# Delta-rule attention with two rational/Mish networks: weight conversion by scaled words in PSUM, and the rest of a redesign around it

## The chip, the cores and the metric

The kernel runs on one core of a Trainium2 chip. A core has TensorE (PE; its weight loads are listed as PEld), VectorE (DVE), ScalarE (ACT), GpSimd (POOL) and SyncE (SP), which issues most of the transfers; each works through its own queue in order. The metric is the device time of one execution in microseconds (us), lower is better. The input arrays lie in DRAM, the weights as 64-bit floats.

## The reference, cut

```python
k_n = k / (norm(k) + 1e-6)                       # B=4, H=8, S=768, D=48
for t in range(S):
    y[t] = q[t] @ state                          # state: 48x48 for each b, h
    state += beta[t] * outer(k_n[t], v[t] - state.T @ k_n[t])
x = y as (3072 tokens, 384)
h = x @ w_in;  P = a0 + a1*h + a2*h^2 + a3*h^3   # w_in 384x2048
x = (P / (1 + |b0|*|h| + |b1|*h^2 + 1e-6)) @ w_out
h = x @ w_in2; out = (h * tanh(log(1 + exp(h)))) @ w_out2
```

## The kernel before, in words

The sequence is cut into 24 chunks `u` of C=32 steps; four chunks make a token group G (0 to 5) of 512 tokens. A chunk needs a prepare: the keys' norms (L259), transposes of k and q (L309, copied at L313), their products (L321) and two masked products on VectorE (L327). For each G one triangular inverse follows for all four chunks: a transpose of `lg` into `xs` (L357), 30 steps of a product and a sum (L366, L372), on VectorE for G=0 and on GpSimd for the others (`ONPOOL`), a transpose into `xt` (L376) and a scaling by beta on GpSimd (L379). Then each chunk has a step: `ks` (L421), `uu` with `xt` (L433), two state products `s_mm(c)` (L450) with a VectorE sum each (L458), `y_mm` (L469), and a product that turns y into the networks' input `x` (L481 to L485). The steps are a chain through the state.

The networks' unit is a slice of 128 of the 2048 hidden columns for 512 tokens: (m, G, f), m the network, f 0 to 15. Each has nine `up` matmuls (L641), elementwise work, and nine `down` (L647; L656 in the last set), 128x128x512 in fp32r with every operand split in a high and a low word, and three products of these. There are 192 units, in sets of 16. In the first network five VectorE operations (L679, L680, L683, L684, L685) and two or three of GpSimd (L674, L678, L687) stand between `up` and `down`; in the second two Mish on ScalarE (L689, L690) and one subtraction on VectorE (L691).

A weight piece is one of 64: two networks, 16 slices, two sides. [...] `st` is stored to a DRAM scratch `wd` (L592) and fetched from there by every unit that needs it (L634), two fetches of 0.393 MB a unit.

The order on every engine is not written by hand. `Plan` collects operations with an estimated duration, the buffers that they read and write, and for units a due time. `order()` works back from the due times to a latest start for each (`late`, less the operation's `early`), then runs a small simulation in which each free engine takes the ready operation with the earliest `late`:

```python
late[j] = min(late[j], late[i] - p[1] - p[4] - self.HOP)
...
pick = min((x for x in queue if x[0] <= t), key=lambda x: (late[x[1]], x[1]))
```

Operations without a due time behind them come in program order. The main function adds the head (group 0's attention, then all conversions) and then sets: first network on G=0; then for g = 0, 1, 2 the steps of g+1, second network on g, prepare of g+2 with its inverse, first network on g+1, norms of g+3; and so on to the second network on the last two groups. `HOST` stretches the due times of units that share the time with steps.

## Time and profile before

| | |
|---|---|
| three runs | 1339.13, 1348.69, 1351.46 us; median 1348.69 |
| profiled execution | time 1342.18 us, span 1340.5 us, mean granted TensorE clock 0.913 |
| busy in the span | PE 1098.8 us (82%), PEld 873.9, DVE 713.5 (53%), ACT 586.1 (44%), POOL 570.8 (43%) |
| moved by transfers | 224.79 MB, mean 168 GB/s |

The span runs from the first to the last instruction of the profiled execution. A row of a window gives the busy time of each engine in that stretch of the span; a row of a line gives the busy time of one line's operations, the mean duration of one, and the idle time of the engine ahead of them with what ended it. A timeline row shows in brackets how long the engine had waited and for whom. PE's busy time counts matmuls in flight, so it is near the span where matmuls follow each other closely.

### The profile page before, as it was taken

The page shows a single profiled execution, that of the slowest core. Times are in us where ns is not written, and L with a number is a line of the kernel's source. Part 1 is how long each engine was busy: PE and PEld are TensorE (multiplying, and loading weights), DVE is VectorE, ACT ScalarE, POOL GpSimd, SP SyncE. Part 2 cuts the span into 40 slices and gives each one's busy share as a digit, 9 for nine tenths or more (in the row PEclk, how much of TensorE's full clock was granted, in tenths as well). Part 3 has the DMA queues.
Part 4 walks back from the last instruction along what each step waited for, and adds up shares of the span by engine and source line. Part 5 has one row for each costly group of instructions (what it writes and reads, how often), then busy time and mean ns, then how long its engine had stood idle before and what let it go on. Part 6 is the DMA issues. An engine that isn't in the chain of part 4 may idle for free.

```text
span 1340.5 us, 32163 instructions
## 1 busy us (share of the span) xinstructions
PE 1098.8 (82%) x13168; PEld 873.9 (65%) x13168; DVE 713.5 (53%) x1172; ACT 586.1 (44%) x1022; POOL 570.8 (43%) x699
## 2 busy tenths in 40 slices
PE   5177558558878899998997998979993799999986
PEld 4175336346666778776776776767772678888775
DVE  3957799987565672227832247631244467841211
ACT  2035456532237572237741267631261457752211
POOL 4123456893115693005891027780037745720000
PEclk9578688869899899999998999899997899999998
DMA  5466777677895666554864554753453346776562
GB/s 100 116 164 175 240 255 244 205 237 222 263 284 165 174 188 163 136 144 105 243 171 108 141 142 115 231 165 97 126 127 104 80 125 166 195 194 191 151 194 64
DMA packets 209283, 224.79 MB, mean 168 GB/s; under 512 B 134864, under 2 KB 147664, under 8 KB 209136
## 3 DMA queue, kind: packets, MB, share of 16 engines
q1 hardware_dynamic: 205616, 222.04, 59.4%
q8 instruction: 104, 1.70, 0.5%
q10 hardware_dynamic: 3264, 0.59, 0.3%
q14 instruction: 43, 0.35, 0.1%
q0 software_dynamic: 256, 0.10, 0.0%
HBM read 190.42 MB, written 29.88 MB: 164 GB/s over the span
## 4 chain that ended last, share of the span: by engine, by line
PE 45%; POOL 10%; DVE 9%; DMA 6%; SPq 6%; ACT 5%; issue 3%; DVEq 0%; POOLq 0%; ACTq 0%
PE b_h L641 18%; PE b_o L647 17%; SPq L719 4%; POOL xs L372 4%; POOL tmp L366 3%; PE b_t L450 3%; PE b_t L469 2%; DMA wd<-st 2%; DMA win<-wd 2%; DMA raw<-in_moe_w_in_dram 1%; PE b_t L433 1%; PE b_o L656 1%; POOL gh L687 1%; DVE b_r L684 1%; DMA out_dram<-ev 1%
## 5 line engine op out<-in xcount | busy, mean ns | idle before, releaser
L641 PE MATMUL b_h<-x,win 128*128 128x512 f32 x1728 | 461.5, 415 | 79.2 <-DVE ms L680 42.6
L647 PE MATMUL b_o<-gh,wout 128*128 128x512 f32 x1584 | 417.8, 411 | 66.2 <-POOL gh L687 41.4
L641 PEld LDWEIGHTS b_h<-x,win 128*128 128x128 f32 x1728 | 334.6, 198 | 165.0 <-DVE ms L680 50.8
L647 PEld LDWEIGHTS b_o<-gh,wout 128*128 128x128 f32 x1584 | 302.7, 196 | 145.2 <-POOL gh L687 49.2
L689 ACT ACTIVATE gh<-b_h 128x512 fp32r<-128x512 f32 x96 | 57.4, 598 | 272.3 <-PE b_h L641 266.7
L691 DVE TENSOR_TENSOR gh<-mq,gh 128x512 fp32r<-128x512 f32 x96 | 69.5, 728 | 179.9 <-ACT mq L690 177.2
L678 POOL TENSOR_TENSOR mq<-mq,mr 128x512 f32<-128x512 f32 x96 | 125.6, 1308 | 87.6 <-ACT mr L676 80.0
L687 POOL TENSOR_TENSOR gh<-mq,gh 128x512 fp32r<-128x512 f32 x96 | 125.1, 1304 | 65.2 <-ACT gh L686 51.0
L579 POOL TENSOR_TENSOR st<-wm,st 128x384 fp32r<-128x384 f32 x64 | 68.5, 1077 | 119.6 <-ACT st L576 100.2
L337 POOL TENSOR_TENSOR mb<-beta_t,mask 128x256 f32<-128x256 f32 x24 | 16.6, 690 | 241.4 <-DVE lg L327 241.2
L683 DVE SCALAR_TENSOR_TENSOR mq<-mq,b_r 128x512 f32<-128x512 f32 x96 | 65.4, 682 | 59.6 <-ACT b_r L682 57.0
L672 ACT ACTIVATE mq<-b_h 128x512 f32<-128x512 f32 x96 | 57.0, 593 | 90.8 <-PE b_h L641 64.0
L679 DVE TENSOR_TENSOR ms<-ms,b_h 128x512 f32<-128x512 f32 x96 | 65.2, 679 | 47.4 <-ACT ms L677 46.8
L372 POOL TENSOR_TENSOR xs<-xs,tmp 128x30 f32<-128x30 f32 (+9 forms) x150 | 82.0, 547 | 11.8
L670 ACT ACTIVATE mr<-mq,cst 128x512 f32<-128x512 f32 x96 | 69.1, 721 | 29.1 <-POOL mq L678 28.8
L366 POOL TENSOR_TENSOR tmp<-xs 128x30 f32<-128x30 f32 (+9 forms) x150 | 77.6, 518 | 8.6
L677 ACT ACTIVATE ms<-b_h,ab 128x512 f32<-128x512 f32 x96 | 73.9, 770 | 0.6 <-PE b_h L641 0.6
L680 DVE SCALAR_TENSOR_TENSOR ms<-ms,ab,b_h 128x512 f32<-128x512 f32 x96 | 71.2, 742 | 1.7
L684 DVE SCALAR_TENSOR_TENSOR b_r<-ms,ab,b_r 128x512 f32<-128x512 f32 x96 | 71.8, 748 | 0.0
L682 ACT ACTIVATE b_r<-mr 128x512 f32<-128x512 f32 x96 | 57.5, 599 | 28.8 <-DVE mq L685 27.7
L576 ACT CAST st<-wm 128x384 fp32r<-128x384 f32 x64 | 32.3, 509 | 80.4 <-DVE wm L569 48.6
L686 ACT CAST gh<-mq 128x512 fp32r<-128x512 f32 x96 | 58.7, 612 | 19.3 <-DVE mq L685 19.0
(124 smaller groups left out, 1350.0 us busy)
## 6 DMA issues: line engine op xcount, KB each, us to landing
win<-wd SPq DMA_DIRECT2D x192, 384.0 KB
wout<-wd SPq DMA_DIRECT2D x192, 384.0 KB
wd<-st SPq DMA_DIRECT2D x64, 384.0 KB
raw<-in_moe_w_out_dram SPq DMA_DIRECT2D x32, 384.0 KB
raw<-in_moe_w_in_dram SPq DMA_DIRECT2D x16, 384.0 KB
v<-in_v_dram SPq DMA_DIRECT2D x192, 24.0 KB
qn<-in_q_dram SPq DMA_DIRECT2D x92, 48.0 KB
kn<-in_k_dram SPq DMA_DIRECT2D x88, 48.0 KB
```

What stands on the lines that cost most here:

```text
L366: eng.tensor_tensor(out=tv, in0=xs[:, j, j + 1:C].unsqueeze(1).to_broadcast([128, j, n]), in1=xs[:, 0:j, j:j + 1].to_broadcast([128, j, n] ...
L372: eng.tensor_tensor(out=xs[:, 0:j, j + 1:C], in0=xs[:, 0:j, j + 1:C], in1=tv, op=ALU.add)
L579: nc.gpsimd.tensor_tensor(out=st[:, 1], in0=mf, in1=st[:, 0].bitcast(F32), op=ALU.subtract)
L641: nc.tensor.matmul(out=h, lhsT=win[:, a, j], rhs=x[:, c, slab[j]], start=n == 0, stop=n == 8)
L647: nc.tensor.matmul(out=self.banks[f"o{d}"], lhsT=wout[:, a, d], rhs=gh[:, c], start=first and j == 0, stop=last and j == 2,)
L670: act(out=r, in_=q, func=ACTF.Ln, bias=k["c"])
L677: p.add("ACT", 775, lambda: act(out=s, in_=h, func=ACTF.Identity, scale=k["a3"], bias=k["a2"]), [hb], [sb])
L678: p.add("POOL", 1335, lambda: P.tensor_tensor(out=q, in0=q, in1=r, op=ALU.mult), [rb], [qb])
L680: p.add("DVE", 750, lambda: V.scalar_tensor_tensor(out=s, in0=s, scalar=k["a1"], in1=h, op0=ALU.add, op1=ALU.mult), [hb], [sb])
L684: p.add("DVE", 750, lambda: V.scalar_tensor_tensor(out=rp, in0=s, scalar=k["a0"], in1=rp, op0=ALU.add, op1=ALU.mult), [sb], ["r"])
L687: p.add("POOL", 1320, lambda: P.tensor_tensor(out=gh[:, 1], in0=q, in1=gh[:, 0].bitcast(F32), op=ALU.subtract), [qb], [ghb])
L691: p.add("DVE", 755, lambda: V.tensor_tensor(out=gh[:, 1], in0=q, in1=gh[:, 0].bitcast(F32), op=ALU.subtract), [qb], [ghb])
```

## The change

**Pieces.** A piece's sign is made without taking it off and putting it back: the high word, read as a 32-bit float, is clamped on both sides, scaled by 2^-112 on ScalarE, and VectorE takes the maximum of the clamped word times -2^-80 and the scaled one. For a positive word that is the scaled one, for a negative one a positive number whose exponent is 32 higher; a shift left by three then moves that bit to the sign's place (`sign`, `shift`), and `tail` brings the low word's top bits. ScalarE's absolute value, VectorE's mask and one two-tensor operation go, the scaled word lies in a PSUM bank. `kind` says which way a piece goes: pieces without "v" are clamped on GpSimd and get their low part from two TensorE matmuls with an identity and its negative (`lo_mm`) and a ScalarE copy; pieces with "v" are clamped on VectorE, into the bank, and get the low part on GpSimd. The `fold` branch of `plan` (ScalarE's parametric ReLU) is not taken: every `kind` has an "m".

**Where pieces stand.** Twelve slices (`HEAD`) of the first network are converted in the head in bank `r`, four more and four of the second network (`EARLY`) in bank `t1` beside the first set, the rest in bank `r` beside the second set. Units 0 to 7 of the first set and all of the second read the converted tiles where they are made; only units 8 to 11 (`FETCHED`) and all later groups fetch them. Fetches fall from 384 to 328.

**Attention.** For G=0 the k part of the prepares stands ahead of the q part, the inverse works in a pair of PSUM banks (`solved`), and the state accumulates in PSUM so that ScalarE copies replace VectorE sums. For all groups `s_mm` is one group of 64 matmuls over four tile positions. The scaling by beta is split in four, one for each chunk. For G of 1 or more the inverse is planned a stage ahead of `finish`, which transposes and scales.

**Planner.** `HOP` depends on the engine, a TensorE change from small to wide tiles costs 150 ns in the plan, the first set's pace is 6500 ns, and GpSimd's and the steps' `early` differ for groups 0 and 1.

In the diff, cut to its core, removed lines that the listing above shows are left out.

```diff
+HEAD = 12
+FETCHED = range(8, 12)
+EARLY = 4
...
-RAW = 3
+RAW = 5
...
-    HOP = 110
+    HOP = {"PE": 180}
...
+            if "k" in what:
+                self.inverse(p, G)
+            if what == "k":
+                self.finish(p, G)
+                p.add("DVE", 980, lambda: self.nc.vector.memset(self.pair, 0.0), (), ["o0", "o1"])
...
+    def solved(self, G):
+        return (self.xs, ["xs"]) if G else (self.pair.rearrange("p (a b) -> p a b", a=C), ["o0", "o1"])
...
+    def finish(self, p, G):
...
+        def scale(g):
+            part = xt[:, g * M:g * M + M]
+            beta = self.beta_t[:, GU * G + g].unsqueeze(2).to_broadcast([128, M, C])
+            return lambda: eng.tensor_tensor(out=part, in0=part, in1=beta, op=ALU.mult)
+        p.add("DVE", 2070, last, xb, [f"xt{g}" for g in range(GU)], early=lead(AHEADX, G))
+        for g in range(GU):
+            p.add(engine, 690 if engine == "POOL" else 350, scale(g), (), [f"xt{g}"], early=lead(AHEADX, G))
...
+        def s_mm():
+            for m in range(M):
+                a, n = divmod(m, 4)
+                for e in (0, 3, 1, 2):
+                    r = self.srow(e)
+                    rows = slice(32 * e, 32 * e + 32)
+                    nc.tensor.matmul(
+                        out=self.banks[bs[e % 2]][r:r + 64, m * D:(m + 1) * D],
+                        lhsT=kn[rows, 2 * n + r // 64, :] if a == e // 2 else kns[rows, n, :],
+                        rhs=U[rows, m, :], start=G > 0, stop=True, skip_group_check=G == 0,
+                    )
...
+            p.add("PE", 1000, s_mm, ["U", knb, knsb], bs, early=lead(AHEAD, G))
             for c in range(2):
...
+                if G:
+                    p.add("DVE", 560, s_out(c), [bs[c], f"{sb}{c}"], [f"{tb}{c}"], early=lead(AHEAD, G))
+                else:
+                    p.add("ACT", 490, s_copy(c), [bs[c]], [f"{tb}{c}"], early=lead(AHEAD, G))
...
+        def clamp():
+            (nc.vector if "v" in kind else nc.gpsimd).tensor_scalar(
+                out=at, in0=high.bitcast(F32), scalar1=self.MOST, scalar2=-self.MOST, op0=ALU.min, op1=ALU.max,
+            )
...
+        def scale():
+            nc.scalar.activation(out=to, in_=at, func=ACTF.Identity, scale=self.DOWN)
+        def sign():
+            nc.vector.scalar_tensor_tensor(out=pv, in0=at, scalar=self.SIGN * self.DOWN, in1=to, op0=ALU.mult, op1=ALU.max)
         def shift():
             nc.vector.tensor_scalar(
...
+                out=ps, in0=ps if kind else m, scalar1=3, scalar2=None, op0=ALU.logical_shift_left,
+            )
+        def tail():
             nc.vector.scalar_tensor_tensor(
...
+                out=m, in0=low, scalar=29, in1=ps, op0=ALU.logical_shift_right, op1=ALU.bitwise_or,
...
+        def lo_mm():
+            nc.tensor.matmul(out=rest, lhsT=self.ident, rhs=v, start=True, stop=False)
+            nc.tensor.matmul(out=rest, lhsT=self.minus, rhs=split[:, 0].rearrange("p k c -> p (k c)"), start=False, stop=True)
+        def lo_copy():
+            nc.scalar.copy(out=split[:, 1].rearrange("p k c -> p (k c)"), in_=rest)
         p.dma(380 if side or self.n else 2500, 384, get, (), [rawb])
+        here, there = (bank, mb) if "v" in kind else (mb, bank)
+        if "v" in kind:
+            p.add("DVE", 520, clamp, [rawb], [here])
+        else:
+            p.add("POOL", 1490, clamp, [rawb], [here])
         if late:
...
+            p.add("ACT", 550, scale, [here], [there])
+            p.add("DVE", 580, sign, [mb], [bank])
+            p.add("DVE", 470, shift, (), [bank])
         else:
...
+        p.add("DVE", 550, tail, [rawb, bank], [mb])
+        p.add("ACT", 510, hi, [mb], [buf])
+        if "v" not in kind:
+            p.add("PE", 1000, lo_mm, [mb, buf], ["h1"], early=3000)
+            p.add("ACT", 520, lo_copy, ["h1"], [buf])
+        else:
+            p.add("POOL", 1060, lo, [mb], [buf])
+        p.dma(380, 384, lambda: nc.sync.dma_start(out=self.scratch[f][:, side], in_=split.bitcast(F32)), [buf], [f"wd{self.n}_{f}_{side}"])
...
+        if G or i in FETCHED:
+            p.dma(330, 384, fetch(0, win), [f"wd{m - 1}_{f}_0"], [winb], early=6000)
+            p.dma(330, 384, fetch(1, wout), [f"wd{m - 1}_{f}_1"], [woutb], early=6000)
...
+    def units(m, g, host, convert=lambda f: None):
+        nonlocal due
         for f in range(NF):
...
+            convert(f)
+            ml.plan_unit(plan, m, g, NG, f, NF, due)
+            due += (PACE if due > START + NF * PACE1 - 1 else PACE1) + HOST * host
+    def first(f):
+        for n in range(HEAD if f == 0 else 0):
+            ml.convert(plan, 1, n, "r", NF, SIGNS)
+        if 0 <= f - 5 < NF - HEAD:
+            ml.convert(plan, 1, HEAD + f - 5, "t1", NF, SIGNS + "v")
+        if 0 <= f - 12 < EARLY:
+            ml.convert(plan, 2, f - 12, "t1", NF, SIGNS + "v")
+    def second(f):
+        for n in (range(EARLY, 6) if f == 0 else (f + 5,)):
+            if n < NF:
+                ml.convert(plan, 2, n, "r", NF, "mv")
+    def prepare(g):
+        at.norms(plan, g)
+        at.prepares(plan, g)
+    units(1, 0, 0, first)
+    at.prepares(plan, 1)
+    at.finish(plan, 1)
+    at.norms(plan, 2)
+    for g in range(NG - 2):
+        at.steps(plan, g + 1)
+        units(2, g, 1, second if g == 0 else lambda f: None)
+        if g == 0:
+            at.prepares(plan, 2)
+        at.finish(plan, g + 2)
+        if g + 3 < NG:
+            at.norms(plan, g + 3)
+            at.prepares(plan, g + 3)
         else:
...
+            at.steps(plan, g + 2)
+        units(1, g + 1, g + 2 == NG - 1)
+    units(1, NG - 1, 0)
+    units(2, NG - 2, 0)
+    units(2, NG - 1, 0)
```

**Three places in the order.** On TensorE where the first `up` stands (`u_151` and `u_168` are the attention's U, `b_h` the networks' banks, `win` the weight tile). Before:

```order
L450 MATMUL b_o_101<-u_151,kns_137 64x48
L450 MATMUL b_o_101<-u_151,kn_127 64x48
L641 MATMUL b_h_98<-x_173,win_176 128x512 x9
L309 MATMUL b_t_105<-ident_120,kn_129 128x2x64 x4
L641 MATMUL b_h_99<-x_173,win_177 128x512 x9
L421 MATMUL b_t_104<-su_149,kq_142 32x48 x32
```

In the changed kernel the end of the fourth step's product into `x` comes first, then (`arena` and `gh` hold a piece's word and its parts):

```order
L543 MATMUL b_t_103<-ident_143,y_176 128x2x64 x2
L547 MATMUL b_t_103<-ident_143,y_176 64x64 x4
L658 MATMUL b_h_99<-arena,ident_143 128x384
L659 MATMUL b_h_99<-gh_133,minus 128x384
L353 MATMUL b_t_102<-ident_143,kn_147 128x2x64 x4
L760 MATMUL b_h_98<-x_112,win_115 128x512 x9
L658 MATMUL b_h_99<-arena,ident_143 128x384
L659 MATMUL b_h_99<-gh_134,minus 128x384
L353 MATMUL b_t_102<-ident_143,qn_148 128x2x64 x4
L658 MATMUL b_h_99<-arena,ident_143 128x384
L659 MATMUL b_h_99<-gh_135,minus 128x384
L760 MATMUL b_h_99<-x_112,win_116 128x512 x9
```

The `up` at L760 now has 22 pairs of `lo_mm` (L658, L659) ahead of it and two more pairs between the first and the second `up`; before it followed the step directly, with the first transposes of the next group behind it.

On VectorE in the middle of the second network's first set (`wm` and `raw` are the piece's tiles, L691 is a unit's subtraction). Before:

```order
L549 TENSOR_SCALAR wm_113<-raw_110 128x384
L554 TENSOR_SCALAR wm_113<-wm_113 128x384
L559 TENSOR_SCALAR wm_113<-wm_113 128x384
L564 SCALAR_TENSOR_TENSOR wm_113<-raw_110,wm_113 128x384
L569 SCALAR_TENSOR_TENSOR wm_113<-raw_110,wm_113 128x384
L549 TENSOR_SCALAR wm_114<-raw_111 128x384
L554 TENSOR_SCALAR wm_114<-wm_114 128x384
L559 TENSOR_SCALAR wm_114<-wm_114 128x384
L564 SCALAR_TENSOR_TENSOR wm_114<-raw_111,wm_114 128x384
L569 SCALAR_TENSOR_TENSOR wm_114<-raw_111,wm_114 128x384
L691 TENSOR_TENSOR gh_195<-mq_185,gh_195 128x512
```

The changed kernel there (L624 clamp, L635 sign, L638 shift, L643 tail, L811 the unit's subtraction, L444 a transpose of the inverse):

```order
L624 TENSOR_SCALAR b_r<-arena 128x384
L444 STREAM_TRANSPOSE xt_173<-xs_172 128x32x32
L635 SCALAR_TENSOR_TENSOR b_r<-b_r,arena 128x384
L638 TENSOR_SCALAR b_r<-b_r 128x384
L643 SCALAR_TENSOR_TENSOR arena<-arena,b_r 128x384
L624 TENSOR_SCALAR b_r<-arena 128x384
L635 SCALAR_TENSOR_TENSOR b_r<-b_r,arena 128x384
L638 TENSOR_SCALAR b_r<-b_r 128x384
L643 SCALAR_TENSOR_TENSOR arena<-arena,b_r 128x384
L624 TENSOR_SCALAR b_r<-arena 128x384
L811 TENSOR_TENSOR gh_137<-mq_123,gh_137 128x512
L635 SCALAR_TENSOR_TENSOR b_r<-b_r,arena 128x384
```

A piece has four operations where it had five, all through one bank `b_r`, and a clamp often stands directly ahead of the sign of the same piece, with ScalarE's scaling between them.

On GpSimd around the inverse of group 5 (L366 and L372 its steps, L687 the low part `gh` that a `down` reads). Before, its end:

```order
L366 TENSOR_TENSOR tmp_157<-xs_155 128x58
L372 TENSOR_TENSOR xs_155<-xs_155,tmp_157 128x29x2
L366 TENSOR_TENSOR tmp_157<-xs_155 128x30
L372 TENSOR_TENSOR xs_155<-xs_155,tmp_157 128x30
L687 TENSOR_TENSOR gh_194<-mq_186,gh_194 128x512
L687 TENSOR_TENSOR gh_195<-mq_187,gh_195 128x512
L379 TENSOR_TENSOR xt_156<-xt_156,beta_t_123 128x1024
```

The changed kernel, the start of group 5's inverse:

```order
L807 TENSOR_TENSOR gh_137<-mq_124,gh_137 128x512
L807 TENSOR_TENSOR gh_133<-mq_125,gh_133 128x512
L807 TENSOR_TENSOR gh_134<-mq_126,gh_134 128x512
L413 MEMSET xs_172 128x32
L419 TENSOR_TENSOR tmp_174<-xs_172 128x30
L425 TENSOR_TENSOR xs_172<-xs_172,tmp_174 128x30
L419 TENSOR_TENSOR tmp_174<-xs_172 128x58
```

Before, two `gh` of units and the scaling L379 stand behind the last of the 60 operations, which began at L360 among the units; now the three last `gh` of the set (L807) stand ahead of the first, and behind the last come only four quarter scalings (L449) and the next set.

## Rows read from the trace of the kernel before

**Rows 1.** Windows by stage: window, us, busy PE, PEld, DVE, ACT, POOL; clock, DMA, GB/s.

```profile
0.00:113.30 113.30, 61.94 (x1760) 54.76 (x1760) 68.87 (x161) 28.63 (x59) 30.77 (x60) 0.74 0.55 129
113.30:264.60 151.30, 97.14 (x571) 69.43 (x568) 133.78 (x198) 83.96 (x154) 92.08 (x92) 0.82 0.76 231
264.60:409.60 145.00, 108.93 (x1742) 83.07 (x1742) 98.73 (x178) 48.71 (x91) 61.59 (x75) 0.87 0.81 252
409.60:503.40 93.80, 82.03 (x452) 64.28 (x453) 64.23 (x98) 63.04 (x101) 72.80 (x89) 0.95 0.60 169
503.40:714.70 211.30, 193.31 (x2331) 153.51 (x2329) 93.96 (x145) 96.22 (x164) 98.85 (x130) 0.97 0.59 156
714.70:908.70 194.00, 175.56 (x2189) 138.54 (x2185) 86.98 (x138) 89.58 (x152) 87.02 (x110) 0.97 0.57 150
908.70:1053.40 144.70, 113.31 (x1915) 88.00 (x1914) 44.14 (x70) 44.89 (x77) 50.41 (x80) 0.88 0.41 108
1053.40:1262.40 209.00, 208.70 (x1947) 169.65 (x1940) 113.39 (x171) 118.04 (x202) 77.30 (x66) 1.00 0.61 168
1262.40:1340.50 78.10, 57.85 (x283) 52.63 (x281) 9.45 (x14) 13.03 (x24) 0.00 (x0) 0.90 0.44 129
```

**Rows 2.** Waits from 113 to 265 us: engine, line, releaser; sum, count, longest (us).

```profile
PE b_h L641 <- DVE ms L680: 33.2, 12, 6.7
```

**Rows 3.** Timeline: start us, us, engine, line; in brackets wait and releaser.

```profile
713.24 1.50 PE L433 MATMUL b_t<-r,xt 32*32 32x48 f32 x64 [6.90 <-POOL xt L379]
...
1046.47 6.19 PE L647 MATMUL b_o<-gh,wout 128*128 128x512 f32 x16 [27.00 <-POOL gh L687]
```

**Rows 4.** Lines of the conversion: busy us, mean ns; idle before, releaser.

```profile
L564 DVE SCALAR_TENSOR_TENSOR wm<-raw,wm 128x384 int32<-128x384 int32 x64 | 50.1, 784 | 2.1 <-DMA raw<-in_moe_w_in_dram 0.4
L569 DVE SCALAR_TENSOR_TENSOR wm<-raw,wm 128x384 int32<-128x384 int32 x64 | 47.5, 748 | 1.6
L554 DVE TENSOR_SCALAR wm<-wm 128x384 f32<-128x384 f32 x64 | 36.5, 570 | 19.7 <-ACT wm L551 18.9
L559 DVE TENSOR_SCALAR wm<-wm 128x384 int32<-128x384 int32 x64 | 32.5, 507 | 2.0
L551 ACT ACTIVATE wm<-raw 128x384 f32<-128x384 f32 x44 | 23.7, 551 | 33.2 <-DMA raw<-in_moe_w_out_dram 19.6 <-DMA raw<-in_moe_w_in_dram 8.0 <-POOL st L579 3.7
L549 DVE TENSOR_SCALAR wm<-raw 128x384 int32<-128x384 int32 x20 | 10.2, 512 | 13.4 <-DMA raw<-in_moe_w_in_dram 6.6 <-POOL st L579 4.2 <-DMA raw<-in_moe_w_out_dram 2.6
```

**Rows 5.** Lines of the first network's VectorE operations, the longest and shortest of five.

```profile
L684 DVE SCALAR_TENSOR_TENSOR b_r<-ms,ab,b_r 128x512 f32<-128x512 f32 x96 | 71.8, 748 | 0.0
L679 DVE TENSOR_TENSOR ms<-ms,b_h 128x512 f32<-128x512 f32 x96 | 65.2, 679 | 47.4 <-ACT ms L677 46.8
```

**Rows 6.** Lines of the inverse on GpSimd, groups 1 to 5.

```profile
L372 POOL TENSOR_TENSOR xs<-xs,tmp 128x30 f32<-128x30 f32 (+9 forms) x150 | 82.0, 547 | 11.8
L366 POOL TENSOR_TENSOR tmp<-xs 128x30 f32<-128x30 f32 (+9 forms) x150 | 77.6, 518 | 8.6
```

**Rows 7.** Timeline of the head: a load's issues, both transposes, first `uu`.

```profile
10.35 7.55 SPq L205 DMA_DIRECT2D v<-in_v_dram  x16
...
37.44 1.94 DVE L357 STREAM_TRANSPOSE xs<-lg 128x1024 f32<-128x1024 f32 x1
...
61.38 2.01 DVE L376 STREAM_TRANSPOSE xt<-xs 128x1024 f32<-128x1024 f32 x1
...
65.43 1.50 PE L433 MATMUL b_t<-r,xt 32*32 32x48 f32 x64 [25.72 <-POOL xt L379]
```

**Rows 8.** Window of one L450 group alone, then timeline rows of TensorE.

```profile
560.30:561.43 1.13, 1.06 (x32) 1.01 (x32) 1.00 0.64 247
...
565.58 0.88 PE L469 MATMUL b_t<-su,kq 64*32 64x48 f32 x64
...
567.21 2.34 PE L647 MATMUL b_o<-gh,wout 128*128 128x512 f32 x9
...
1154.25 4.24 PE L647 MATMUL b_o<-gh,wout 128*128 128x512 f32 x18
```

389 lines of the change are left out of this document (197 added, 192 removed).

## Prediction

> **What bounds the kernel now.** I read the busy time by stage first. I cut the span where a set of sixteen units begins or ends, because the stages have different limits [rows 1]. In the order of the nine rows they are: the head up to the first unit (113.3 us); first network, token group 0 (151.3); second network, group 0 (145.0); first network, group 1 (93.8); three stretches of 211.3, 194.0 and 144.7 us, each with attention steps; the units from 1053 us on (209.0); and the last set with its stores (78.1). They add up to 1340.5. TensorE is full in the eighth row alone, 208.7 of 209.0 us. Two units' nine-matmul halves take 4.24 us there with a tail of 0.16, so a unit costs 4.08 us and a set of sixteen 65 [rows 8]. Set beside that, the second and third rows hold 151 and 145 us for sixteen units each.
>
> The second row is VectorE's: it is busy 133.8 of 151.3 us, 88%. The unit's five operations lie between 0.679 and 0.748 us [rows 5], about 3.54 us together, so 16 units are 57 us. A weight piece takes four operations of 0.570, 0.507, 0.784 and 0.748 us [rows 4], together 2.61, and 27 pieces stand in this stretch of the order: 70 us. The sum, 127, is nearly all of the 133.8. The waits say the same: TensorE's next `up` waited 33.2 us for `ms` of L680 [rows 2]. The third row is not VectorE's (98.7 of 145.0 busy); there the transfers run at 252 GB/s with a mean share of 0.81 on the DMA engines, 36.5 MB. From the fifth row on TensorE is the limit except where the next group's inverse on GpSimd is late: `uu` waited 6.90 us for `xt`, and at 1046 us a `down` waited 27.00 us behind 60 inverse operations that stood ahead of its `gh` [rows 3].
>
> **The change, part by part.** The sum is made against the profiled execution, span 1340.5 us and time 1342.2; the median of the three runs is 1348.7, half a per cent above.
>
> *A piece on VectorE.* Abs, the two-sided clamp, the sign and its mask go. What is left is sign, shift and tail, with a clamp of its own only in the 40 "v" pieces; GpSimd clamps the other 24. No trace row has these operations on a PSUM bank. Nearest are the same shapes in SBUF: 0.784 and 0.748 for the two-tensor ones, 0.507 for the shift, 0.512 for reading every second word of `raw` [rows 4]. The five unit operations have a PSUM operand and are 128x512 wide at 0.679 to 0.748 [rows 5]; three quarters of that is 0.51 to 0.56. So sign and tail lie between 0.51 and 0.78, and I take 0.66: 1.83 us a piece without clamp (1.5 to 2.1), 2.34 with it (2.0 to 2.6). ScalarE takes 0.551 for such a pass [rows 4], and its scaling stands between clamp and sign, so VectorE waits about 0.65 us where nothing else is placed there.
>
> *Head.* By VectorE's order six pieces now stand ahead of the first inverse, six inside it and 13 behind it up to the first unit; before, 11 in all. Inside, 6 x 1.83 is 11 us. Before, the inverse began with one transpose at 37.44 and ended at 61.38 with the other, of 2.01 us [rows 7]. It can begin earlier, since only four masked products are ahead of it and not eight; what holds it is piece six, whose load is SP's 46th issue. Sixteen issues took 7.55 us [rows 7], 0.47 each, so it leaves at 22 us and is converted by about 30. The `uu` behind it then comes at 30 + 24 + 11 + 2 and some 3 that I allow for two ScalarE copies and the first quarter of the scaling: 70, against 65.43. From there to the first `up` it was 113.3 - 65.4 = 47.9 us [rows 1, 7] for four steps; each step loses one of two state products and its hop, some 1.5 us, and I take 44. The first unit is also queued behind 22 pieces' `lo_mm`; the 22nd load is issue 192, which is 91 us plus about 8 to land and convert: not later. VectorE's own work behind the inverse is 13 pieces, 24 us, plus some 13 us of sums and products: not later either. So 114 us, no gain, from 104 (the inverse starts early and all else is hidden) to 128 (every load waits a little).
>
> That upper end also covers a cost on TensorE: a wide half unit beside small tiles takes 2.34 us where a dense one takes 2.04 [rows 8], and the 22 `lo_mm` pairs put wide work among small tiles; 22 x 2 x 0.25 is 11 us if all of it were on the chain. The Trainium skill, "TensorEngine Tiling (Array Packing)", Key Properties, has it that changing the tiling mode drains the engine; by that rule the head would be 125 us and the total 11 us more. The row bears it out in kind; how much of it is on the chain no row here shows.
>
> *First network, group 0.* Nine pieces are left: 57 + 9 x 1.83 + 8 x 0.51 + 5 for norms and products is 83 us of VectorE. At the same 88% it is 94 us, and I take 97 for the longer first fill; 90 to 110. Nothing is fetched for the first eight units, which read the converted tiles where they lie.
>
> *Second network, group 0.* 30 pieces x 2.34 is 70 us, plus what VectorE did beside its 26 pieces before (98.7 - 26 x 2.61 - 20 x 0.512 = 21), plus 12 places where clamp and sign stand back to back (8 us): 99. At 88% that is 113. The transfers lose 32 fetches of 0.393 MB (128 x 768 words), 12.6 of 36.5 MB; 23.9 MB at 252 GB/s is 95 us, so they no longer end last. 113; 100 to 130.
>
> *First network, group 1.* TensorE's rows: 297 matmuls at 4.08 / 18 = 0.227 are 67 us; seven product groups and thirteen groups of transposes for token groups 2 and 3, none longer than the 0.88 of a group of 64 [rows 8], 17 at most; a start and some switches 4: 88 (before 93.8); 84 to 94.
>
> *From there to the last set* (211.3 + 194.0 + 144.7 + 209.0 = 759.0 us; TensorE busy 690.9). The state product `s_mm` becomes one group over four tile positions instead of two groups over two. One old group is 1.06 us for 32 matmuls; `y_mm` has four positions and does 64 in 0.88 [rows 8]. So 2.13 becomes between 0.88 and 2.13; I take 0.9, as the neighbouring groups show, for 16 steps: 20 us. Group 3's products are moved up a stage: 9 us. The inverse of the next group now stands behind the last `gh` of a set and ahead of a set of the second network that does not use GpSimd. It takes 30 x (0.518 + 0.547) = 32 us [rows 6] against 65 us and more of TensorE work, and its result lies in `xs` until `finish`. The tightest is group 2: 21 of its steps, 22 us, the transpose and the scaling, about 26 in all, against seven `up`, five `down` and three small groups, 27: at most a few us late. So the waits of 6.90 and 27.00 go, and so does the slow restart behind them. 690.9 - 20 - 9 is 662, and for idle left over I take 16: 678 (650 to 712).
>
> *Last set:* 78, unchanged.
>
> Sum: 114 + 97 + 113 + 88 + 678 + 78 = 1168 us, on the profiled execution's scale, where time was 1.7 above span. I forecast **1168 us**, 13% below.
>
> **The rivals.**
> 1. *The one bank serializes.* All pieces of the head share `b_r`, those of the third stretch too: scale, sign, shift and tail must be through before the next enters. Free of waits that is 0.55 + 1.83, with the clamp 2.9 us. But the queues are in order, and a `scale` behind a waiting Mish holds the bank. Before, a piece took 151.3 / 27 or 145.0 / 26 = 5.6 us. If each still held its bank so long, 22 pieces behind a 12 us start are 135 and 30 pieces 168: 1168 + 21 + 55 = **1244**. Against it: before had three private `wm` buffers and its limit was VectorE's sum and the transfers, which both fall.
> 2. *The same bank, ending slower.* 52 pieces are in question; from 5.6 us on each further us costs 52. It decides from (1342 + 13 - 1244) / 52 = 2.1 more: from 7.7 us a piece the kernel ends at **1355** or later. That needs each piece to wait some 5 us; VectorE's longest run without a piece inside the inverse is about seven steps, 5 us, so it can happen to a few pieces, not to most.
> 3. *The inverse stays late:* the four stretches keep 759.0 - 20 or so: 1168 + 61 = **1229**. For it: GpSimd was busy 98.85 us in the fifth stretch [rows 1] and is not relieved. Against: its inverse is behind the units, no longer among them.
> 4. *Everything fits*: lower ends of head and first two sets and half of the idle: **1105**.
>
> **How the numbers follow.** Forecast 0.70, rival 1 0.12, rival 3 0.07, rival 4 0.08, rival 2 0.03. The range 1105 to 1225 holds the forecast, most of rival 4 and the nearer part of 1 and 3, about 8 in 10. One per cent, 13 us, is about what a measurement of this kernel can tell from no change. Slower only by rival 2: 0.03; within 1% 0.01; faster 0.96.
>
> **What would show it.** First `up` between 104 and 128 us; the second stretch at 90 to 110 with VectorE over 80% busy; the third at 100 to 130 with the DMA share well under 0.8; no wait over 3 us for `xt` or a `gh` behind the inverse; `s_mm` at 64 matmuls in about 0.9 us; sign and tail at 0.5 to 0.78 us. Wrong would be: a third stretch over 140 with VectorE waiting on ScalarE's scale (rival 1), `up` after 130, or `uu` waiting for `xt` again (rival 3).

## The result, and the profile after

The changed kernel takes 1232.76 us (median of four runs, 1230.75 to 1234.06) against 1343.91 before: ratio 0.917 (95% interval 0.911 to 0.923), faster by 8%. The forecast was 1168, with a range to 1225: the direction is right, the size is not. The profiled execution has a span of 1228.9 us. Its stages, as the windows of the changed kernel by stage (columns as in [rows 1]):

```profile
0.00:137.60 137.60, 87.15 (x2077) 68.61 (x2078) 82.69 (x190) 51.30 (x117) 30.80 (x66) 0.84 0.61 163
137.60:228.50 90.90, 80.78 (x584) 63.42 (x583) 82.49 (x142) 71.20 (x127) 61.79 (x58) 0.97 0.58 169
228.50:348.60 120.10, 98.56 (x1598) 73.83 (x1596) 92.58 (x163) 57.17 (x113) 66.78 (x97) 0.91 0.73 227
348.60:441.00 92.40, 86.62 (x860) 69.03 (x863) 63.72 (x100) 65.83 (x108) 63.70 (x74) 0.98 0.60 163
441.00:1130.00 689.00, 648.48 (x8094) 518.78 (x8084) 337.62 (x515) 350.97 (x589) 330.82 (x413) 0.97 0.60 159
1130.00:1228.90 98.90, 77.48 (x368) 68.91 (x366) 14.83 (x22) 18.55 (x34) 0.00 (x0) 0.90 0.46 132
```

| stage (us) | before [rows 1] | forecast | after | after less forecast |
|---|---|---|---|---|
| head | 113.3 | 114 | 137.6 | +23.6 |
| first network, group 0 | 151.3 | 97 | 90.9 | -6.1 |
| second network, group 0 | 145.0 | 113 | 120.1 | +7.1 |
| first network, group 1 | 93.8 | 88 | 92.4 | +4.4 |
| all behind it | 837.1 | 756 | 787.9 | +31.9 |
| sum | 1340.5 | 1168 | 1228.9 | +60.9 |

So the head, forecast as no gain, became 24 us longer, and the long middle gave back 49 us where 81 were forecast. The operations of a piece have the durations that were bounded (0.5 to 0.78): lines of the changed kernel, columns as in [rows 4], pieces without VectorE's clamp first.

```profile
L635 DVE SCALAR_TENSOR_TENSOR b_r<-arena,b_r 128x384 f32<-128x384 f32 x24 | 13.3, 555 | 23.8 <-ACT b_r L632 23.7
L638 DVE TENSOR_SCALAR b_r<-b_r 128x384 int32<-128x384 int32 x48 | 27.1, 564 | 1.3
L643 DVE SCALAR_TENSOR_TENSOR arena<-arena,b_r 128x384 int32<-128x384 int32 x48 | 26.5, 552 | 2.6
L624 DVE TENSOR_SCALAR b_r<-arena 128x384 f32<-128x384 f32 x24 | 13.4, 560 | 0.7
```

That is 1.67 us a piece without clamp and 2.23 with it (1.83 and 2.34 taken). The idle time ahead of the first line's 24 `sign`, 23.7 us spent waiting for ScalarE's scaling, points at the head, where these pieces are made.

**The head.** Waits of the changed kernel from 76 to 138 us (columns as in [rows 2]), then its timeline (columns as in [rows 3]):

```profile
ACT b_r L632 <- POOL arena L624: 25.4, 7, 5.2
POOL arena L624 <- DMA arena<-in_moe_w_in_dram: 20.1, 3, 9.9
POOL arena L624 <- DMA arena<-in_moe_w_out_dram: 18.3, 4, 6.7
PE b_h L658 <- ACT x L662: 4.7, 3, 1.8
PE b_h L658 <- ACT gh L662: 3.3, 1, 3.3
```

```profile
77.37 0.88 PE L496 MATMUL b_t<-r,xt 32*32 32x48 f32 x64 [2.65 <-DVE xt L449]
...
105.02 4.74 SPq L242 DMA_DIRECT2D v<-in_v_dram  x8
109.87 1.48 SPq L610 DMA_DIRECT2D arena<-in_moe_w_out_dram  x1
...
114.74 0.36 SPq L610 DMA_DIRECT2D arena<-in_moe_w_out_dram  x1
```

ScalarE's scaling waits for GpSimd's clamp, and that for the load of the weights; the attention's copies stand behind the scaling in ScalarE's queue. TensorE waits 8.0 us ahead of `lo_mm` (L658), with the steps' small products behind it in its order. The last row is the 22nd load: it leaves at 114.7 us, where the forecast had 91. SyncE issues nearly without a pause from the start to 137 us. The eight loads of `v` in this row take 4.74 us, 0.59 each.

**The middle.** Three rows of the changed kernel's timeline and, behind them, three from its later part:

```profile
462.56 0.61 POOL L382 TENSOR_TENSOR mb<-beta_t,mask 128x256 f32<-128x256 f32 x1
463.21 0.42 DVE L371 TENSOR_TENSOR lg<-b_t,mb 128x256 f32<-128x256 f32 x1 [9.36 <-POOL mb L382]
463.69 1.11 PE L353 MATMUL b_t<-ident,kn 128*128 128x128 f32 x4 [7.61 <-DVE lg L371]
...
899.82 0.32 SPq L753 DMA_DIRECT2D wout<-wd  x1
900.60 28.30 SPq L839 DMA_DIRECT2D out_dram<-ev  x48
932.27 4.18 PE L760 MATMUL b_h<-x,win 128*128 128x512 f32 x9 [8.33 <-DMA win<-wd]
```

The waits of [rows 3] are gone, and two others are there. At 463 us TensorE stands 7.61 us behind VectorE's `lg`, which needs `mb`, a product of GpSimd that now stands behind the inverse. At 932 us it waits 8.33 us for a weight tile whose fetch stands in SyncE's queue behind 48 output stores, 28.3 us of issues.

### The profile page after: what moved, and what is told of

The parts are those of the page before. It is cut to its first block, busy times and chain, and to the rows that moved or that the text cites. A ratio compares the mean times of both kernels' runs of the same rounds, so it can differ in the third digit from the quotient of the medians.

```text
span 1228.9 us, 32934 instructions
## 1 busy us (share of the span) xinstructions
PE 1079.1 (88%) x13560; PEld 862.6 (70%) x13560; DVE 673.9 (55%) x1128; ACT 615.0 (50%) x1085; POOL 553.9 (45%) x705
## 3 DMA queue, kind: packets, MB, share of 16 engines
q8 instruction: 107, 1.75, 0.6%
## 4 chain that ended last, share of the span: by engine, by line
PE 52%; SPq 12%; POOL 9%; DVE 9%; DMA 7%; issue 5%; ACT 5%; DVEq 0%; POOLq 0%; ACTq 0%
PE b_h L760 22%; PE b_o L766 19%; SPq L839 6%; POOL xs L425 3%; POOL tmp L419 3%; DMA kn<-in_k_dram 2%; PE b_t L531 2%; PE b_o L775 2%; PE b_t L510 1%; DVE mq L803 1%; DVE b_r L804 1%; DMA win<-wd 1%; DMA out_dram<-ev 1%; DVE mq L805 1%; PE b_t L496 1%
## 5 line engine op out<-in xcount | busy, mean ns | idle before, releaser
L760 PE MATMUL b_h<-x,win 128*128 128x512 f32 x1620 | 417.8, 404 | 31.3 <-DMA win<-wd 14.7
L766 PE MATMUL b_o<-gh,wout 128*128 128x512 f32 x1476 | 378.5, 403 | 19.5 <-DMA wout<-wd 9.4
L760 PEld LDWEIGHTS b_h<-x,win 128*128 128x128 f32 x1620 | 305.5, 193 | 105.2 <-issue 18.0
L766 PEld LDWEIGHTS b_o<-gh,wout 128*128 128x128 f32 x1476 | 279.4, 193 | 85.0 <-DMA wout<-wd 10.0
L811 DVE TENSOR_TENSOR gh<-mq,gh 128x512 fp32r<-128x512 f32 x96 | 74.8, 780 | 194.3 <-ACT mq L810 182.8
L807 POOL TENSOR_TENSOR gh<-mq,gh 128x512 fp32r<-128x512 f32 x96 | 123.8, 1291 | 73.0 <-ACT gh L806 71.1
L799 DVE TENSOR_TENSOR ms<-ms,b_h 128x512 f32<-128x512 f32 x96 | 65.4, 682 | 60.9 <-ACT ms L797 58.6
L792 ACT ACTIVATE mq<-b_h 128x512 f32<-128x512 f32 x96 | 56.9, 592 | 62.6 <-PE b_h L760 60.8
L803 DVE SCALAR_TENSOR_TENSOR mq<-mq,b_r 128x512 f32<-128x512 f32 x96 | 65.6, 683 | 37.4 <-ACT b_r L802 33.5
L805 DVE SCALAR_TENSOR_TENSOR mq<-mq,b_r 128x512 f32<-128x512 f32 x96 | 65.7, 685 | 2.6
L794 POOL TENSOR_SCALAR mr<-mq,ab 128x512 f32<-128x512 f32 x48 | 37.0, 771 | 59.3 <-ACT mq L792 59.3
L810 ACT ACTIVATE mq<-b_h 128x512 f32<-128x512 f32 x96 | 57.0, 594 | 2.4 <-PE b_h L760 2.4
```

Of the source, the lines that this page charges most:

```text
L760: nc.tensor.matmul(out=h, lhsT=win[:, a, j], rhs=x[:, c, slab[j]], start=n == 0, stop=n == 8)
L766: nc.tensor.matmul(out=self.banks[f"o{d}"], lhsT=wout[:, a, d], rhs=gh[:, c], start=first and j == 0, stop=last and j == 2,)
L803: p.add("DVE", 685, lambda: V.scalar_tensor_tensor(out=q, in0=q, scalar=1.0 + 1e-6, in1=rp, op0=ALU.add, op1=ALU.mult), ["r"], [qb])
L805: p.add("DVE", 690, lambda: V.scalar_tensor_tensor(out=q, in0=q, scalar=2.0, in1=rp, op0=ALU.subtract, op1=ALU.mult, reverse0=True), ["r"] ...
L807: p.add("POOL", 1320, lambda: P.tensor_tensor(out=gh[:, 1], in0=q, in1=gh[:, 0].bitcast(F32), op=ALU.subtract), [qb], [ghb])
L811: p.add("DVE", 755, lambda: V.tensor_tensor(out=gh[:, 1], in0=q, in1=gh[:, 0].bitcast(F32), op=ALU.subtract), [qb], [ghb])
```

## The experiments

Every run was timed in three rounds; the numbers are medians, to be set against 1232.8. First `up` is where the head ends. The kernel before had medians of 1338 to 1344 us beside the groups of runs, so a difference of some 5 us tells little.

### SyncE's queue in the head

`one_load`, one transfer for an input-side piece instead of seven:

```diff
-            elif self.n:
+            elif True:
                 nc.sync.dma_start(out=raw, in_=self.w_in.rearrange("(k p) f -> p k f", p=128)[:, :, cols])
```

> Each of the first network's input-side pieces is loaded by one transfer instead of seven, in the order of the rows as they lie (so the rows of these weights are permuted and the result is another); the planned order is the same. Theory: SyncE's queue sets the head. In the changed kernel SyncE issues without a pause from 0 to 137 us, and the 22nd load leaves at 115 us where 91 were forecast. 72 issues fewer at about 0.6 us take 43 us from it, more than the 23 by which the first `up` is late (137 against 114), so the attention's chain takes over: first `up` at 105 to 118 us and the kernel 18 to 30 us shorter, about 1205 to 1215. Rival: the head is late because ScalarE and TensorE mix pieces with small tiles (the order on the engines); then the first `up` stays at 130 or later and the time within 6 us of 1232.8.

Measured 1207.9; first `up` at 121.7 us, the first `uu` at 65.5 instead of 77.4. 25 us less, 16 of them in the head: SyncE's queue holds it. The first `up` is 4 us later than expected. From the first `uu` to it TensorE waits for no piece any more, but stands 14 us in four stops without a releaser, which the last section reads.

`after_pool`, the loads of v and q of group 0 from GpSimd's queue, nothing else:

```diff
-        p.dma(8 * 400, 300, lambda: self.load_v(u), (), [vb], early=lead(AHEAD, G))
+        p.dma(8 * (550 if u < GU else 400), 300, lambda: self.load_v(u, nc.gpsimd if u < GU else nc.sync), (), [vb], early=lead(AHEAD, G), engine="POOL" if u < GU else "SP")
```

(and the same for `load_q`).

> The loads of v and q of token group 0 (48 transfers) are issued from GpSimd's queue instead of SyncE's; all else is the changed kernel, with the correct rows. Theory: SyncE's queue sets the head; 48 issues at about 0.6 us are 29 us less in its queue, of which the one-load run gave back 16 us of a first `up` at 137: first `up` at 118 to 128 us, time 1213 to 1224. Rival: GpSimd's own queue passes the delay on, since its clamps stand behind the loads that it issues and those behind buffers that come free late: first `up` stays at 132 or later, time within 5 us or longer.

Measured 1218.8, first `up` at 122.4, both as the theory had them. Two edits that have only SyncE's issues in common shorten the head alike.

`lo_pool`, the low parts of the head's pieces by GpSimd, `if "v" not in kind:` replaced by `if False:`.

> The low parts of the 24 pieces of the head are made by GpSimd (1.06 us each, 25 us in all, where it is busy 31 of 136 us) instead of two TensorE matmuls and a ScalarE copy. The prediction allowed up to 11 us of the head for wide matmuls among small tiles. Theory A: that cost is on the chain (TensorE stood at 1.5 to 4.7 us behind `lo_mm` and ScalarE's copy several times): first `up` at 120 to 132, time 1217 to 1228. Theory B: the loads decide the head, so the first `up` stays at 134 or later and the time within 5 us of 1232.8.

Measured 1240.1. The head gets 10 us shorter (first `up` at 127.7) and the two sets behind it 10 and 9 us longer, as GpSimd's queue is later there. So the TensorE low parts do cost about 10 us of the head, and the edit moves them elsewhere. The 10 us are not the price of wide matmuls among small ones alone: with `lo_mm` go the 8.0 us of waits for late pieces ahead of it, TensorE's own time for it and ScalarE's copies.

### The output stores

`st590`, the store's cost and due time in the plan:

```diff
-                    p.dma(340, 40, lambda n=n, d=d, ev=ev: self.store(G, d, ev, n), [evb], (), due=due + (LAG + 4) * PACE)
+                    p.dma(590, 40, lambda n=n, d=d, ev=ev: self.store(G, d, ev, n), [evb], (), due=due + (LAG + 8) * PACE)
```

> In the plan, an output store costs 590 ns instead of 340 (48 of them took 28.3 us in the trace) and its due time is four paces later; nothing else is changed, so that the fetches of weights stand between the stores and not behind them. Theory: the waits for `win` and `wout` (8.3, 3.9, 3.9, 1.5 us and the slow clock behind them) go: 8 to 20 us shorter, 1213 to 1225. Rival: the stores become later instead, the two `ev` buffers are free later and `down` waits for `ev` by as much; then within 5 us of 1232.8 or slower.

Measured 1190.0, 43 us less: twice the expected gain, and more than the forecast's whole error in the middle. Its timeline at the same stores:

```profile
878.06 9.47 SPq L839 DMA_DIRECT2D out_dram<-ev  x16
887.64 2.21 SPq L753 DMA_DIRECT2D win<-wd  x2
889.94 5.23 SPq L839 DMA_DIRECT2D out_dram<-ev  x9
895.27 0.41 SPq L753 DMA_DIRECT2D wout<-wd  x1
```

The fetches now stand between the stores. From 349 us on every set gets shorter, by 3 to 12 us, the last set included, but for the two that TensorE fills. TensorE's idle time from the first network's end on group 1 to 78 us before the end of the span (441 to 1150.8 us, here 439 to 1111.3) falls from 40.5 to 19.4 us, which is half of the gain. The order of TensorE changes with the plan, so what part of the rest is a better mix is not told apart; nor is the share of the cost from that of the due time.

`before_st590`, the same two numbers in the kernel before.

> The kernel before the change, with the output stores planned at 590 ns and four paces later, nothing else. Question: were the stores ahead of the fetches already a cost of the kernel before, which the prediction's 759 us carried along unseen, or did the change bring them? Theory: they were there too, since its 48 stores a group stand in SyncE's queue in the same way: 15 to 40 us less, 1300 to 1325. Rival: there the fetches were hidden behind the waits for GpSimd, under 8 us less.

Measured 1316.2 against 1344.5: 28 us (ratio 0.981, 0.977 to 0.985), as the theory had it. So a cost of this kind was in the kernel before too, and the 759 us of the forecast carried it along. In the changed kernel the same edit gives 43; where the other 15 come from no run shows.

### The product behind the inverse, and the inverse

`mb_dve`:

```diff
+            mon, meng, mns = ("DVE", nc.vector, 430) if u >= 3 * GU else ("POOL", nc.gpsimd, 620)
             p.add(
-                "POOL", 620, lambda: nc.gpsimd.tensor_tensor(
+                mon, mns, lambda: meng.tensor_tensor(
                     out=mb,
```

> The product beta times mask (`mb`) of token groups 3 to 5 is made on VectorE instead of GpSimd, where it stands behind the 32 us of the inverse of group 2. Theory: TensorE's wait of 7.6 us for `lg` at 456 us and the slower clock behind it (the stretch 441 to 541 us has 90.9 us busy where the one of the same work at 809 us has 81.9) go together: 1232.8 becomes 1215 to 1224. Rival: the wait only moves to `xt`, since the inverse itself is late by as much; then within 4 us.

Measured 1222.1, as the theory had it; the set from 441 us on gets 8 us shorter and the one with the next steps 2. The wait for `mb` was a price of the earlier inverse.

`inv_late`, `self.inverse` called at the start of `finish` for groups 3 to 5.

> The inverse of groups 3, 4 and 5 is planned directly ahead of its transposition and scaling, as before the change, not a stage earlier. Theory: the waits of before come back (6.9 us for `xt`, 27 us for `gh` behind the 60 operations, and the slow clock behind them), less the 7.6 us that `lg` waits now for a product queued behind the early inverse: 15 to 35 us more, 1248 to 1268. Rival: in the new order the inverse fits in beside the units without being early, and what helped is something else: within 6 us of 1232.8.

Measured 1234.9, but this run says nothing of the inverse: the planner sorts by due time, and the operations of TensorE, VectorE, ScalarE and GpSimd come in the same order as in the changed kernel. It shows instead what the same program measures a second time: 2 us more. So `prep_late` moves the prepares themselves back a stage:

```diff
-        if g == 0:
-            at.prepares(plan, 2)
+        at.prepares(plan, g + 2)
         at.finish(plan, g + 2)
-            at.norms(plan, g + 3)
-            at.prepares(plan, g + 3)
...
         units(1, g + 1, g + 2 == NG - 1)
+        if g + 3 < NG:
+            at.norms(plan, g + 3)
```

> The prepares of groups 3 to 5 are planned where the kernel before had them, directly ahead of the inverse's transposition and one stage later than in the changed kernel; this time the order on GpSimd does change (the inverses stand among units again, the last one among those of the first network on group 4). Theory: that is what took the waits of 6.9 and 27 us away; they come back, less the 7.6 us that `lg` waits in the changed kernel: 15 to 35 us more, 1248 to 1268. Rival: with the other changes to the order the inverses fit in there as well, within 6 us of 1232.8.

Measured 1242.3, 10 us more and not 15 to 35. The last two stages with steps get 9 and 17 us longer (the second taken with the set behind it), the second network on group 1 gets 10 shorter (the wait for `mb` is gone), and no wait of 27 us comes back; the longest is 12.3 us for `win`, behind the stores again. The earlier prepare with its inverse is a gain, about 10 us net.

### The state product

`s_two`, the loop over `m` inside a loop over the two halves, `for e in (c, 2 + c)`.

> The state product is issued as two groups of 32 matmuls over two tile positions each, one behind the other, as before the change; all else is the changed kernel. Theory: the one group over four positions saves about 1.2 us for each of 16 steps behind the second stage and four in it, 19 to 24 us in all: 1250 to 1257. Rival: the steps lie beside units, so TensorE's time for them is hidden by waits anyway: under 6 us more.

Measured 1234.8, 2 us more: the rival. A line of the changed kernel and the same of this one, columns as in [rows 4] (busy time of 19 steps):

```profile
L510 PE MATMUL b_t<-u,kn 32*64 32x48 f32 x608 | 22.5, 221 | 2.1 <-ACT u L502 1.9
```

```profile
L510 PE MATMUL b_t<-u,kn 32*64 32x48 f32 x608 | 36.5, 222 | 1.9 <-ACT u L502 1.9
```

From the first start to the last end a step's 64 matmuls take 1.15 us in the changed kernel and 1.88 here (medians of 23), 0.73 less and not 1.2: two groups back to back overlap, which two separate groups of 1.06 did not show. Sixteen steps make 12 us of TensorE; the 2 that are seen in the time are within the noise.

### The pieces

`old_pieces`, the five operations of before in the changed kernel's places:

```diff
+        p.add("ACT", 550, mag_o, [rawb], [mb])
+        p.add("DVE", 400, size_o, (), [mb])
+        p.add("DVE", 430, shift_o, (), [mb])
+        p.add("DVE", 640, sign_o, [rawb], [mb])
+        p.add("DVE", 640, low_o, [rawb], [mb])
```

> The changed kernel with the pieces made as before: absolute value on ScalarE, two-sided clamp, shift, sign and low word on VectorE in the private buffer, no clamp on GpSimd and no PSUM bank; places, low parts and all else are those of the changed kernel. Theory (the prediction's VectorE sums): a piece costs VectorE 2.61 us again, 0.9 more for the 9 in the first set and 0.3 to 0.5 more for the 30 in the second network's first set, nothing in the head, which waits for loads: 8 to 20 us more, 1240 to 1253. Rival 1 of the prediction (the one bank holds the pieces back): the second network's first set gets shorter by 5 us or more and the time is 1232 or less. Third way: VectorE has room in both stages, within 5 us of 1232.8.

Measured 1265.5, 33 us more: 10 in the first set, 29 in the second network's first set, some of it taken back behind. `old_wm4` is the same with `WM = 4`.

> The run with the old pieces, with four private buffers for a piece instead of three. The old pieces cost 33 us where VectorE's sum gave 8 to 20; 29 of them fell in the second network's first set, where VectorE's four operations took 2.47 us a piece against 2.24 of the new ones, 7 us in 30 pieces. Theory A: the other 22 us are buffers: an old piece holds its buffer from the absolute value to the low part, the new one lies in the PSUM bank for the first half of its way; a fourth buffer then takes back 10 us or more, 1243 to 1255 against 1265. Theory B: it is the order on the engines (absolute values on ScalarE and low parts on GpSimd stand in queues behind attention's work); a fourth buffer changes under 5 us.

Measured 1264.5: not the buffers (theory A falls). TensorE's timeline in `old_pieces`:

```profile
292.13 1.65 PE L769 MATMUL b_h<-x,win 128*128 128x512 f32 x3 [11.69 <-POOL win L653]
```

There group 2's inverse starts on GpSimd at 269 us and runs 22 us in one piece ahead of the next `lo`; in the changed kernel it starts at 232 and is mixed with them. To tell VectorE's time from this order, `half_dve` leaves it as it is and shortens three operations:

```diff
-            nc.vector.scalar_tensor_tensor(out=pv, in0=at, scalar=self.SIGN * self.DOWN, in1=to, op0=ALU.mult, op1=ALU.max)
+            nc.vector.scalar_tensor_tensor(out=pv[:, 0:192], in0=at[:, 0:192], scalar=self.SIGN * self.DOWN, in1=to[:, 0:192], op0=ALU.mult, op1=ALU.max)
```

(the same in `shift` and `tail`).

> Sign, shift and tail of every piece cover only the first half of the columns (the other half of each weight piece is left unconverted), with the same order and the same waits; each takes about 0.28 us instead of 0.56, so a piece takes 0.84 us less of VectorE. Theory (VectorE's sum bounds both stages, as the prediction had it): 17 pieces in the first set and 30 in the second network's first set, 7 and 20 us less, time 1205 to 1212. Rival (the pieces' way through ScalarE and GpSimd and the loads bound the second, where VectorE is 77% busy): 5 to 8 us in the first set, under 6 in the other, 1219 to 1228.

Measured 1231.9, less of a gain than even the rival expected: nothing. Its windows of the two sets:

```profile
137.60:228.50 90.90, 81.34 (x536) 63.44 (x534) 76.17 (x140) 72.17 (x130) 60.92 (x57) 0.96 0.57 170
228.50:350.00 121.50, 97.83 (x1665) 73.44 (x1666) 76.53 (x166) 57.66 (x114) 67.47 (x98) 0.93 0.74 228
```

VectorE is busy 76.2 and 76.5 us instead of 82.5 and 92.6, and both sets last as long as before. `extra_dve` goes the other way, `for _ in range(2):` around the tail.

> Every piece's tail is done twice on VectorE (the second leaves the same words), in the same planned order: 0.55 us more of VectorE a piece, the other side of the run with half the columns, which gave nothing. 17 pieces in the first set make 9 us and 30 in the second network's first set 17 us. Theory A (VectorE is covered in both stages, the price of the old pieces came from another order on GpSimd): under 8 us more, 1233 to 1241. Theory B (VectorE just fits and bounds as soon as it gets longer): 15 to 27 us more, 1248 to 1260, and the 33 us of the old pieces would be VectorE's after all.

Measured 1243.6, 11 us more where VectorE got 26 more in these sets: 3 in the first, 7 in the second network's. Between both theories: VectorE doesn't bound the sets, but has little room left. Of the old pieces' 33 us VectorE's time can be 10 or so; the rest goes with the other order on GpSimd, which no run here took apart further.

### Together

`combo` is `st590` with a third `ev` buffer and `mb_dve`; `combo_pool` has the loads of `after_pool` too; `combo_lop` adds the edit of `lo_pool`, and `combo_kpool` the 16 loads of k of group 1 on GpSimd's queue instead:

```diff
-        self.ev = ring("ev", 2, [128, TOK])
+        self.ev = ring("ev", 3, [128, TOK])
...
+            p.dma(4 * (550 if G == 1 else 450) if G else 10, 300, (lambda u=u: self.load_k(u, nc.gpsimd if G == 1 else None)) if G else lambda: None, (), [xb], early=lead(AHEADP, G), engine="POOL" if G == 1 else "SP")
```

> The store cost of 590 ns in the plan, a third `ev` buffer, and the `mb` products of groups 3 to 5 on VectorE, together. Theory: the gains add, since they are in different places (the stores alone gave 43 us, `mb` alone 11; in the run with the stores' cost TensorE still waits 5.9 us for `lg`): 1190 less 7 to 12, and up to 3 for the third buffer: 1174 to 1184. Rival: both moved the same wait, then 1186 to 1192.

> The combined kernel (stores at 590 ns, third `ev` buffer, `mb` of groups 3 to 5 on VectorE) with the loads of v and q of group 0 issued by GpSimd. Theory: the two gains lie in different stages, 1184 less the 12 to 16 us of the head: 1166 to 1174, which is the forecast's 1168 with both of its errors taken out. Rival: the plan of the head shifts and the gain is lost behind: 1178 to 1186.

> The best version so far (1173.5) with the low parts of the head's pieces on GpSimd instead of TensorE and ScalarE. Once the loads are less in the way, GpSimd's clamps wait 29 us for `lo_mm` of an earlier piece (three private buffers), so theory: the head gets 5 to 10 us shorter, 1163 to 1169. Rival: GpSimd's queue, with loads, clamps and low parts in order, is later than TensorE's: no gain or longer.

> The best version so far (1173.5) with the 16 loads of k of group 1 on GpSimd's queue too. Theory: SyncE's queue still paces the head at a first `up` of 127; 16 issues at 0.6 us are 10 us less: 1163 to 1170. Rival: the chain of steps and pieces has taken over (pieces wait for `lo_mm`, 29 us of waits on GpSimd), within 4 us of 1173.5.

Measured 1184.0, 1173.5, 1178.8 and 1166.8. The gains add for the most part (43 and 11 alone are 49 together; the loads' 14 are 11 on top); GpSimd's low parts lose again; and 16 issues fewer in SyncE's queue still shorten the head (first `up` at 126.2, then 120.5). `combo_kpool` has a ratio of 0.870 (0.866 to 0.873) to the kernel before and is the fastest. Its head and first set, windows as above:

```profile
0.00:120.40 120.40, 79.39 (x2077) 62.49 (x2078) 81.42 (x190) 51.93 (x116) 66.35 (x130) 0.91 0.73 187
120.40:213.00 92.60, 81.33 (x591) 62.55 (x588) 83.09 (x143) 71.37 (x128) 62.31 (x58) 1.00 0.55 168
```

## Why the prediction was wrong in size, step by step

*Head (forecast 114, measured 137.6): the step that failed* is "the 22nd load is issue 192, which is 91 us plus about 8 to land and convert: not later". It was issue 192, but it left at 114.7. The 0.47 us an issue came from one row of sixteen [rows 7]. The usual issue does take that long: from one start to the next the median of the 192 is 0.48. But 18 of them took 0.8 to 2.0 us, 23.8 in sum, and 11 pauses of the queue took 5.3 more, so that the mean was 0.60. What makes an issue that long no row shows. The first `up` stands behind 22 `lo_mm`, and so behind these loads; `one_load` and `after_pool` shorten the head by 16 and 15 us and have only the issues taken out of this queue in common. The inverse was late by the same cause (its first transpose begins at 36.9 us where 30 was taken, `uu` comes at 77.4 instead of 70, and at 65.5 in `one_load`).

A second term of the head failed too: "I take 44" from `uu` to the first `up`. It was 60.3, of which TensorE waits 8.0 for pieces and 8.7 in five stops without a releaser; with SyncE relieved it is 56.2 (`one_load`) and 50.5 (`after_pool`), so 44 was reached in no run. The bound of 11 us for wide matmuls among small ones stands on a misreading: the half unit's 2.34 holds the tail of 0.16 that had been taken off the dense one's 2.04, so that the rows give 0.14 a half unit and not 0.30 [rows 8]. The 10 us of `lo_pool` hold the waits for pieces and so don't bear it out. The Trainium skill's "TensorEngine Tiling (Array Packing)", Key Properties, which the prediction had cited, says that a change of tiling mode drains the engine and gives no price; no run here measures one.

*First network, group 0 (forecast 97, measured 90.9) and second network, group 0 (113, 120.1):* both inside their ranges, but for another reason than given. "At the same 88%", VectorE's busy share, was the basis; `half_dve` shows that VectorE's time does not bound them, so the fit is luck. In the first TensorE is busy 80.8 of 90.9 us. In the second no engine is full (TensorE 98.6 of 120.1 at a granted clock of 0.91, VectorE 92.6). Of TensorE's 21.5 idle us there 11.2 end with a high or low part of a piece (L650, L653) and 6.1 with a step's `x` (L556); what makes the pieces late stays open. That the transfers no longer end last there agrees with the rows: the share is 0.73 instead of 0.81, and no wait of TensorE there ends with a transfer.

*First network, group 1 (88, 92.4):* inside its range; TensorE waits 2.7 us for `ev` and 3.0 for weight tiles, which are the stores again, and `st590` takes 3 us off.

*All behind it (756, 787.9):* with the last 78.1 us cut off as before, the stretch from 441 us takes 709.8 where 678 were forecast; TensorE is busy 669.3 (662 forecast) and idle 40.5 (16). Two terms were wrong and one was taken without a reason. (1) The state products, 20 us, were priced from single groups; they are 0.73 us a step, 12 us of TensorE, and no more than 2 us of the time. (2) "So the waits of 6.90 and 27.00 go, and so does the slow restart behind them": they went, but the prepare's `mb` was left behind the inverse in GpSimd's queue, a wait of 7.6 us that cost about 10 (`mb_dve`), and the whole move is worth about 10 us net (`prep_late`). (3) The 16 us "for idle left over" come from no row. SyncE's queue was not read in these stages at all; its stores, 28 us a group, hold the fetches. With them mended the idle time is 19.4 and the kernel 43 us faster (`st590`).

*The rivals.* The one bank (1, 2) did not hold the pieces back: the 30 of the second network's first set took 120.1 us, 4.0 each where rival 1 had 5.6, and without the bank (`old_pieces`) the set is longer. The late inverse (3) gives 1229 and so nearly the measured number, by chance: `xt` was late for no step of groups 1 to 5. Nothing fitted like (4), and its 1105 does not follow from its parts: 10, 7 and 13 us of lower ends and half of the 16 make 1130. What happened was none of them.

Added up: with the stores, `mb` and 48 loads mended and a third `ev` buffer the kernel takes 1173.5 us, 5 from the forecast. So these are together as large as its error; that they are all of it is not shown, and that the two numbers meet is in part luck, since the stores' edit also gives back time that the forecast had taken over from before.

## What to carry to other kernels

Count the issues of the queue that starts the transfers, stage by stage, with each form's own duration, and ask what stands behind every long run of small ones: here planning 48 small stores at their true time, and later, gave more (43 us) than any other single edit, and a wrong 340 ns in the plan had hidden it. A short row gives the usual issue and not the long ones among many. When work is moved ahead on an engine, look at what was left behind it in the same queue. An engine that is busy 90% of a stage need not bound it (VectorE in the first set, `half_dve`): make its work shorter in the same order before the sum is built on it.

## What the runs showed that was not expected

The usual issue on SyncE costs by its form, and not by its size. In the changed kernel the median of a fetch of 384 KB is 0.32 us, of a load of `v` of 24 KB 0.43, of an output store of 16 KB 0.54; with the pause to the next a store makes 0.59 (28.30 / 48).

And TensorE stops in the middle of a group of small matmuls with no semaphore to wait for; in `one_load`:

```profile
73.71 0.20 PE L531 MATMUL b_o<-u,am 32*32 32x48 f32 x1 [3.62 <-issue]
...
80.73 0.29 PE L365 MATMUL b_t<-kq 64*32 64x32 f32 x4 [2.92 <-issue]
```

63 matmuls of the first group and 60 of the second ran before these rows. The transfers point to what TensorE lacked. One queue carries what the profile calls "instruction"; its row for the whole run of `one_load`, then for 68 to 74 us and for 78.4 to 80.7 (packets, MB, share):

```profile
q8 instruction: 107, 1.75, 0.6%
...
q8 instruction: 1, 0.02, 3.1%
...
q8 instruction: 1, 0.02, 2.6%
```

Each packet has 16 KB, and the 1.75 MB are 65 bytes for each of TensorE's 27,120 matmuls and weight loads. The packets in these two windows end at 72.33 and 79.41 us, 1.4 and 1.3 us before TensorE goes on; the two other long stops of this head (ends at 93.87 and 109.27) follow a packet by 1.5 and 1.4. In all 19 traces, behind the first 20 us, 170 of 173 stops of over 0.9 us without a releaser end 1.0 to 1.7 us behind such a packet, where a time picked at random would do so in 6 of 100 cases (13 in this head). So, as far as rows show, TensorE had run out of instructions and waited for the next 16 KB; no run changed their number to try it. It was so before the change too: 7.7 of the 47.9 us from `uu` to the first `up` were such stops, and the forecast carried them along.
